# A scaled addition on one core: the first load is issued as two halves, on two queues

## The chip, the cores and the metric

The kernel runs on one core of a Trainium2 chip. The metric is the device time of one execution in microseconds (us); lower is better. For comparisons the median of several executions is taken. Besides, one execution was recorded by the hardware profiler; its span runs from the core's first instruction to its last.

## What is computed

```python
B, S, D = 512, 32, 640          # x, fx: bfloat16 of shape (B, S, D); alpha: bfloat16 of shape (1,)

def reference(x, fx, alpha):
    return x + alpha * fx
```

Each of x, fx and the output has 512 x 32 x 640 = 10,485,760 elements, 20.97 MB in bfloat16. So 41.94 MB are read from the device memory (HBM) and 20.97 MB are written.

## The kernel before

The three arrays are looked at as one flat row of elements. With K = 128 elements and P = 128 partitions (the rows of the on-chip memory), the data have 640 blocks of K x P elements, and they are cut into three chunks, of blocks 0 to 254, 254 to 464 and 464 to 640 (`CHUNKS`, L18). Within a chunk each partition holds one contiguous stretch; `rows` (L64) gives the piece of it that belongs to blocks a to b. A transfer of blocks a to b therefore has 128 rows, one for each partition, of (b - a) x 128 x 2 bytes: 8 KiB for blocks 0 to 32, 56,832 bytes for blocks 32 to 254, 65,024 bytes for blocks 0 to 254.

On chip there is a single buffer `buf` of 828 blocks (L77). The pieces of fx and x have fixed places in it (`F` and `X`, L20 and L21; `at`, L83), some of which are used twice, so that a later piece can be loaded only when an earlier one has been used up. One short piece of the product is kept in the accumulator memory (`held`, L78).

The order of the work is written out by hand in `PLAN` (L26 to L49), one step a line, and the loop at L145 issues the steps in that order:

- `f a b` and `x a b` load blocks a to b of fx and x into `buf` (`load_f`, `load_x`, both by `transfer`, L94). Every transfer is issued by the sync engine (SP) on its own DMA queue; L95 is therefore the line of all loads and stores in the profile.
- `a` (L126) loads alpha, spreads it to all partitions with a matmul by ones on TensorE, and copies it to `a_f` on VectorE (L134).
- `m a b` multiplies a piece of fx by alpha in place (VectorE, L111), `p` copies a piece of the product to `held` (L117), `t a b` adds the product to x in place (L124).
- `s a b` stores a finished chunk (SP, L95).

At the top of the plan stand `f 0 32`, the load with the 8 KiB rows, and `f 32 254`, the rest of the first chunk of fx; then alpha, `x 0 254`, `f 254 464` and the first multiply `m 0 254`, which needs both pieces of fx. SP takes its transfers in the order of the plan and waits, before one of them, for the semaphores of what must be over. At the end SP waits for all steps in `done` (L151 to L153).

The change touches the first line of the plan, the functions beside `load_f` and the table `does` (L136).

Of the kernel before, what the change touches and what calls it, by code (L numbers as in the profile page):

```python
# [1 line left out]

# [4 lines left out]

ACT = mybir.ActivationFunctionType
ALU = mybir.AluOpType
F32 = mybir.dt.float32  # L10
BF16 = mybir.dt.bfloat16
U32 = mybir.dt.uint32

K = 128
P = 128


CHUNKS = [(0, 254), (254, 464), (464, 640)]  # L18

F = [(0, 254, 464), (254, 464, 254), (464, 640, 442)]  # L20
X = [(0, 254, 0), (254, 464, 618), (464, 640, 266)]  # L21

HELD = (400, 464)
ALL = 828

PLAN = """  # L26
f 0 32
f 32 254
a
x 0 254  # L30
f 254 464
m 0 254
t 154 254
x 254 464
t 0 154
m 400 464
p 400 464
m 254 400
f 464 640
t 266 400  # L40
x 464 640
m 464 640
t 254 266
t 400 464
s 0 254
t 464 640
s 254 464
s 464 640
"""  # L49
LATE = {"s 0 254": "t 400 464"}  # L50


@with_exitstack
def kernel(
    ctx: ExitStack,
    tc: tile.TileContext,
    x: bass.AP,
    fx: bass.AP,
    alpha: bass.AP,
    out: bass.AP,  # L60
):
    nc = tc.nc

    def rows(t, a, b):  # L64

        flat = t.rearrange("b s d -> (b s d)")
        s, e = next(c for c in CHUNKS if c[0] <= a and b <= c[1])
        v = flat[s * K * P : e * K * P].rearrange("(p n) -> p n", p=P)
        return v[:, (a - s) * K : (b - s) * K]

    consts = ctx.enter_context(tc.tile_pool(name="consts", bufs=1))
    psum = ctx.enter_context(tc.tile_pool(name="psum", bufs=1, space=bass.MemoryType.PSUM))
    whole = ctx.enter_context(tc.tile_pool(name="whole", bufs=1))
    ctx.enter_context(tc.manual_schedule())

    sync = mybir.DependencyInfo(mybir.DependencyClass.Sync, mybir.DependencyReason.DATA)
    buf = whole.tile([P, ALL * K], x.dtype, name="buf")  # L77
    held = psum.tile([P, (HELD[1] - HELD[0]) * K // 2], U32, name="held")  # L78
    done = []
    said = {}  # L80
    lanes = {}

    def at(pieces, a, b):  # L83

        s, _, h = next(p for p in pieces if p[0] <= a < p[1])
        e, _, g = next(p for p in pieces if p[0] < b <= p[1])
        assert h - s == g - e
        return buf[:, (a + h - s) * K : (b + h - s) * K]

    def in_psum(a, b):  # L90
        assert HELD[0] <= a and b <= HELD[1]
        return held[:, (a - HELD[0]) * K // 2 : (b - HELD[0]) * K // 2]

    def transfer(name, out, in_):  # L94
        r = nc.sync.dma_start(out=out, in_=in_)  # L95
        if name in LATE:
            tc.add_manual_dep(r.ins, said[LATE[name]].ins.name, sync, reason="issue late")
        return r

    def load_f(a, b):  # L100
        return transfer(f"f {a} {b}", at(F, a, b), rows(fx, a, b))

    def load_x(a, b):
        return transfer(f"x {a} {b}", at(X, a, b), rows(x, a, b))

    def store(a, b):
        return transfer(f"s {a} {b}", rows(out, a, b), at(X, a, b))

    def multiply(a, b):
        term = at(F, a, b)  # L110
        return nc.vector.tensor_scalar(  # L111
            out=term, in0=term, scalar1=lanes["a_f"][:], scalar2=None, op0=ALU.mult
        )

    def hold(a, b):

        return nc.vector.tensor_scalar(  # L117
            out=in_psum(a, b), in0=at(F, a, b).bitcast(U32), scalar1=0, scalar2=None, op0=ALU.bitwise_or
        )

    def total(a, b):
        s = at(X, a, b)
        term = in_psum(a, b).bitcast(x.dtype) if HELD[0] <= a < HELD[1] else at(F, a, b)
        return nc.vector.tensor_tensor(out=s, in0=s, in1=term, op=ALU.add)  # L124

    def alpha_to_lanes():  # L126
        a_1 = consts.tile([1, 1], alpha.dtype, name="a_1")
        done.append(nc.sync.dma_start(out=a_1[:], in_=alpha[None, :]))  # L128
        ones = consts.tile([1, P], alpha.dtype, name="ones")
        nc.vector.memset(ones[:], 1.0)  # L130
        a_ps = held[:, 0:1].bitcast(F32)
        done.append(nc.tensor.matmul(a_ps, ones[:], a_1[:], start=True, stop=True))  # L132
        lanes["a_f"] = consts.tile([P, 1], F32, name="a_f")
        return nc.vector.tensor_copy(out=lanes["a_f"][:], in_=a_ps)  # L134

    does = {  # L136
        "f": load_f,
        "x": load_x,
        "a": alpha_to_lanes,
        "m": multiply,  # L140
        "p": hold,
        "t": total,
        "s": store,
    }
    for step in PLAN.split("\n"):  # L145
        if step:
            what, *of = step.split()
            said[step] = does[what](*map(int, of))
            done.append(said[step])

    rest = nc.sync.nop(nofuse=True)  # L151
    for i in done[:-1]:
        tc.add_manual_dep(rest.ins, i.ins.name, sync, reason="all but the last store")  # L153


# [1 line left out]
_INS = ['x', 'fx', 'alpha']  # L157
_OUTS = [((512, 32, 640), 'bfloat16')]


# [23 lines left out]
```

## Time and profile before

| | us |
|---|---|
| median of 3 executions | 150.68 (150.58 to 150.79) |
| the profiled execution, its own time | 150.84 |
| its span | 149.1 |
| VectorE (DVE) busy | 70.1 |
| share of the 16 DMA engines' span in packets | 98.0% |
| first load (8 KiB rows): issue by SP begins | 0.72 |
| the same: median from issue to landing | 4.8 |
| first multiply on VectorE begins | 22.70 |
| last store issued | 112.0 |

The page gives for each engine the time in which it executed instructions, for the DMA queues their packets and bytes, and the chain of work that ended last. Issuing a DMA does not count as busy; its queue is shown as SPq. A packet of a transfer is one row of one partition here, and the trace holds a record with start, duration and size for each. The time from issue to landing of a transfer contains its stay behind earlier transfers in the same queue.

### The profile page before, as it was taken

The page shows a single profiled execution, that of the slowest core. Times are in us where ns is not written, and L with a number is a line of the kernel's source. Part 1 is how long each engine was busy: PE and PEld are TensorE (multiplying, and loading weights), DVE is VectorE, ACT ScalarE, POOL GpSimd, SP SyncE. Part 2 cuts the span into 40 slices and gives each one's busy share as a digit, 9 for nine tenths or more (in the row PEclk, how much of TensorE's full clock was granted, in tenths as well). Part 3 has the DMA queues.
Part 4 walks back from the last instruction along what each step waited for, and adds up shares of the span by engine and source line. Part 5 has one row for each costly group of instructions (what it writes and reads, how often), then busy time and mean ns, then how long its engine had stood idle before and what let it go on. Part 6 is the DMA issues. An engine that isn't in the chain of part 4 may idle for free.

```text
span 149.1 us, 80 instructions
## 1 busy us (share of the span) xinstructions
PE 0.2 (0%) x1; PEld 0.1 (0%) x1; DVE 70.1 (47%) x13; POOL 0.2 (0%) x4
## 2 busy tenths in 40 slices
PE   0000000000000000000000000000000000000000
PEld 0000000000000000000000000000000000000000
DVE  0000009940089999999399179949990000000000
POOL 0000000000000000000000000000000000000000
DMA  5979996969969999999988899899696999879984
GB/s 158 611 320 412 488 523 279 558 279 558 452 303 447 462 462 462 462 462 418 430 387 387 387 532 435 387 473 558 279 558 279 510 462 462 390 315 556 399 387 193
DMA packets 1442, 62.92 MB, mean 422 GB/s; under 512 B 162, under 2 KB 162, under 8 KB 162
## 3 DMA queue, kind: packets, MB, share of 16 engines
q1 hardware_dynamic: 1442, 62.92, 98.0%
HBM read 41.94 MB, written 20.97 MB: 422 GB/s over the span
## 4 chain that ended last, share of the span: by engine, by line
DMA 55%; DVE 19%; SPq 1%; issue 0%; DVEq 0%
DMA buf<-in_x_dram 55%; DVE buf L124 19%; SPq L95 1%; SPq L128 0%; DVEq L124 0%
## 5 line engine op out<-in xcount | busy, mean ns | idle before, releaser
L124 DVE TENSOR_TENSOR buf<-buf 128x12800 bf16<-128x12800 bf16 (+4 forms) x5 | 39.1, 7836 | 15.2 <-DMA buf<-in_x_dram 15.2
L111 DVE TENSOR_SCALAR buf<-buf,a_f 128x32512 bf16<-128x32512 bf16 (+3 forms) x4 | 22.2, 5549 | 4.2 <-DMA buf<-in_fx_dram 4.2
L134 DVE COPY a_f<-held 128x1 f32<-128x1 f32 x1 | 0.2, 157 | 21.5 <-PE held L132 21.5
L117 DVE TENSOR_SCALAR held<-buf 128x4096 uint32<-128x4096 uint32 x1 | 4.4, 4428 | 0.0
L124 DVE TENSOR_TENSOR buf<-buf,held 128x8192 bf16<-128x8192 bf16 x1 | 4.4, 4414 | 0.0
L130 DVE MEMSET ones<- 1x128 bf16 x1 | 0.2, 165 | 0.8 <-PEq L168 0.8
L132 PE MATMUL held<-a,ones 1*128 1x1 bf16 x1 | 0.2, 158 | 22.3 <-DMA a<-in_alpha_dram 22.3
L168 POOL MEMSET const-bfloat16-1.0<- 128x1 bf16 x1 | 0.1, 101 | 0.0
L168 POOL MEMSET const-uint8-127<- 128x1 uint8 x1 | 0.1, 101 | 0.0
L132 PEld LDWEIGHTS <-ones 1*128 1x128 bf16 x1 | 0.1, 100 | 1.0 <-DVE ones L130 1.0
L168 POOL MEMSET const-float32-0.0<- 128x1 f32 x1 | 0.1, 98 | 0.2 <-issue 0.2
L168 POOL MEMSET const-float32-1.0<- 128x1 f32 x1 | 0.1, 98 | 0.0
## 6 DMA issues: line engine op xcount, KB each, us to landing
buf<-in_x_dram SPq DMA_DIRECT2D x1, 8128.0 KB, 39.5
out_dram<-buf SPq DMA_DIRECT2D x1, 8128.0 KB, 21.2
buf<-in_fx_dram SPq DMA_DIRECT2D x1, 7104.0 KB, 21.2
buf<-in_fx_dram SPq DMA_DIRECT2D x1, 6720.0 KB, 55.0
buf<-in_x_dram SPq DMA_DIRECT2D x1, 6720.0 KB, 24.8
out_dram<-buf SPq DMA_DIRECT2D x1, 6720.0 KB, 36.6
buf<-in_fx_dram SPq DMA_DIRECT2D x1, 5632.0 KB, 21.1
buf<-in_x_dram SPq DMA_DIRECT2D x1, 5632.0 KB, 17.4
```

The costliest lines, as they stand in the source:

```text
L95: r = nc.sync.dma_start(out=out, in_=in_)
L111: return nc.vector.tensor_scalar(out=term, in0=term, scalar1=lanes["a_f"][:], scalar2=None, op0=ALU.mult)
L117: return nc.vector.tensor_scalar(out=in_psum(a, b), in0=at(F, a, b).bitcast(U32), scalar1=0, scalar2=None, op0=ALU.bitwise_or)
L124: return nc.vector.tensor_tensor(out=s, in0=s, in1=term, op=ALU.add)
L130: nc.vector.memset(ones[:], 1.0)
L132: done.append(nc.tensor.matmul(a_ps, ones[:], a_1[:], start=True, stop=True))
L134: return nc.vector.tensor_copy(out=lanes["a_f"][:], in_=a_ps)
L168: nc = _bacc.Bacc("TRN2", target_bir_lowering=False, num_devices=1)
```

## The change

The first load of the plan becomes a step of its own kind, `2f 0 32`. It issues the rows of partitions 64 to 127 on ScalarE's DMA queue and those of partitions 0 to 63 on the sync engine's, as before. Both are in the list of what SP waits for at the end. The bytes, their places in `buf` and all other steps are the same. ScalarE has no other work in this kernel.

```diff
 PLAN = """
-f 0 32
+2f 0 32
 f 32 254
 a
 x 0 254
...
+    def load_f_by_two(a, b):
+
+        h = P // 2
+        done.append(nc.scalar.dma_start(out=at(F, a, b)[h:], in_=rows(fx, a, b)[h:]))
+        return nc.sync.dma_start(out=at(F, a, b)[:h], in_=rows(fx, a, b)[:h])
+
...
     does = {
         "f": load_f,
+        "2f": load_f_by_two,
         "x": load_x,
```

## The prediction

> **What bounds the kernel now.** I read four views in this order: the page's busy times and DMA parts, the chain that ended last, the waits of SP's queue with the waits of the engines, and the first five microseconds cut into half-microsecond stretches.
>
> From the page:
>
> ```profile
> PE 0.2 (0%) x1; PEld 0.1 (0%) x1; DVE 70.1 (47%) x13; POOL 0.2 (0%) x4
> ...
> q1 hardware_dynamic: 1442, 62.92, 98.0%
> HBM read 41.94 MB, written 20.97 MB: 422 GB/s over the span
> ```
>
> No engine is busy for half of the span, but the 16 DMA engines are, taken together, busy for 98.0% of 149.1 us. The chain of waits starts with SP's issues and then consists of DMA landings, with VectorE between them:
>
> ```profile
> 0.66 0.07 issue
> 0.72 0.38 SPq L95
> ...
> 1.99 39.54 DMA buf<-in_x_dram
> ```
>
> The first transfer is issued 0.72 us after the start. After that the chain is no help for this change: the VectorE steps in it run while the DMA engines work on other transfers. The packet records of the trace say it better. Sorted by their ends, they fall into 16 unbroken strings, one for each DMA engine, and in each the next packet begins within a few ns of the last one's end: 8 rows of 8 KiB, then 8 rows of every later transfer. A 56,832-byte row takes 2.09 us from start to start, a 65,024-byte row 2.40 us, an 8 KiB row 0.306 us. The strings begin between 1.73 and about 2.3 us and end between 147.45 and 147.98 us. So **the time is the start of a string, plus 80 rows at a fixed pace, plus about 2.9 us of landing, wind-up and what lies outside the span** (150.84 us was the profiled execution's own time, against a last end of 147.98). Only what makes a string start later, run slower or stand still can move the end.
>
> The rest of the page bears this out. VectorE first needs the first 8 KiB rows when alpha is there:
>
> ```profile
> PE held L132 <- DMA a<-in_alpha_dram: 22.3, 1, 22.3
> DVE a_f L134 <- PE held L132: 21.5, 1, 21.5
> ...
> SPq L95 <- DVE buf L124: 70.9, 4, 26.1
> ```
>
> Those rows land by 5.54 us (the landing records), so they have 17 us to spare. SP waits 70.9 us for VectorE before later issues, yet no string shows a gap there, so these waits are covered. All these VectorE steps hang on landings, so they move with the strings if these start earlier or later.
>
> What is left is the start. In the stretches the columns are the stretch, its length, four engines, PE's clock, DMA share and GB/s; a packet is counted whole where it begins, which is why shares over 1 occur:
>
> ```profile
> 1.50:2.00 0.50, 0.00 (x0) 0.00 (x0) 0.00 (x0) 0.00 (x0) 1.00 1.30 213
> 2.00:2.50 0.50, 0.00 (x0) 0.00 (x0) 0.00 (x0) 0.00 (x0) 1.00 0.64 115
> 2.50:3.00 0.50, 0.00 (x0) 0.00 (x0) 0.00 (x0) 0.00 (x0) 1.00 0.59 229
> 3.00:3.50 0.50, 0.00 (x0) 0.00 (x0) 0.00 (x0) 0.00 (x0) 1.00 1.00 426
> ```
>
> From 3 us on the rate is 426 GB/s; before that the engines hold packets but move few bytes. In the records the first row of an engine takes 0.37 to 1.29 us, a later one 0.309. Eight rows begun at 1.73 us and at the full pace would be done at 1.73 + 8 x 0.306 = 4.18 us; the strings reach that point between 4.77 and 5.17 us. So **the start loses 0.6 us on the quickest engine and 1.0 us on the slowest**. That is all the change can win.
>
> **The change part by part.**
>
> SP's issue. The number of SP's issues stays 11. The first took 0.378 us for 128 rows and alpha's, of one element, 0.315, so half the rows save 0 to 0.06 us of SP's time. The next issue ended at 1.58 us and its packets began at 4.81 us, behind the first rows: nothing waits for the 0.06 us. I put it at 0.
>
> ScalarE's issue. One instruction of 0.32 to 0.61 us (the range of SP's issues) on an engine that has nothing else; the trace releases ScalarE from the start barrier at 0.66 us, as it does SP. Its rows can therefore begin at about 1.73 us, as SP's. Cost 0.
>
> Completions. Every engine now signs off two transfers instead of one. Such a 4-byte packet takes 9 ns and some 6 ns around it: 0.015 us on every string, on the path.
>
> Waits. The first multiply now waits for two landings instead of one, and SP's last gathering wait for one more. Behind the multiply stands all of VectorE's work, but the cover is 17 us (above). SP's gathering steps take 0.06 us each and are over at 135 us, 13 us ahead of the end. Cost 0; without this cover, 0.06 us.
>
> The start. Two queues may hand the engines their first rows sooner. Bounds: 0 (what is slow at the start is the first read, which stays) and -1.0 us (the slowest engine loses nothing). The spread of the first starts, some 0.5 us, is the only part that shows engines waiting for a row to be handed out; halving it gives about -0.25 us. I take -0.2, the nearest to that row.
>
> Which engine moves which row. This is the part that the diff does not show. Now 128 rows lie on 16 engines, 8 each, and the even pace of all 16 says that none of them stands in another's way. After the change each half has 64 rows; if it is still spread over all 16 engines, each has 4 rows of the lower half and 4 of the upper, so that the 8 partitions which one engine fills now are filled by two. If the place where the rows land takes one row at a time at the present pace, two engines share it while they work on the same half. No row of the trace shows two engines at one place, so I bound it: at best the two alternate (one in the lower half while the other is in the upper) and it costs 0; at worst they stay in step, and each row lasts twice as long: 8 x 0.306 = 2.45 us. The first row is slow anyhow, which leaves 7 x 0.306 = 2.14 us as the usual worst. An engine that starts late by a part of a row stays late by that part, since both lose the same; starts differ by 0 to 0.5 us, thus by anything between no row and a whole one, and the middle is 7 x 0.153 = 1.07 us. The slowest of the 16 sets the end and would lie above the middle; engines that fall out of step on the way would lie below it. I take +1.1.
>
> [...]
>
> Sum: 0 + 0 + 0.015 + 0 - 0.2 + 1.1 = +0.9 us. Against the profiled execution that is 150.84 + 0.9 = 151.74; that execution lies 0.16 us above the median of the runs (150.68), so the forecast for the median is **151.6 us**, +0.6%. With the bounds of the sharing (0.3 to 2.3 us net) the slower case runs from 151.0 to 152.9.
>
> **The rivals.**
>
> A, faster: the start is bound by the handing out of rows, and two queues do it at once. For it: the strings begin up to 0.5 us apart, and one engine or another stands still after its first row (a gap of 0.04 to 0.24 us in the records). Against it: most of the loss sits in the first row's own 0.37 to 1.29 us, and later issues show no such loss. It decides if no two engines get in each other's way. Price: half of the slowest engine's 0.98 us, -0.49: 150.84 - 0.49 = 150.35, or 150.2 beside the median; at most 149.7.
>
> B, no change: the same 16 engines move the same 1 MB at the same pace, and the first read is as slow as now; the second queue only saves issue time that nobody waits for. For it: the string's pace of 0.306 us a row, and 0.98 us at the start of which little is shown to be handing out. Price: +0.015, so 150.7. [...]
>
> C, the second queue comes late: ScalarE's rows appear only after SP's four, and take turns with rows of 56,832 bytes. Nothing stands still, since SP's next issue is queued by 1.58 us; the sharing then touches four rows of an engine: 0 to 4 x 0.306 = 1.22 us, taken in the middle +0.6: 151.3.
>
> **How the numbers follow.** A measurement of this kernel can tell about 0.2% (0.3 us) from no change, so same is 150.38 to 150.98. Forecast (sharing outweighs the start) 0.55, all of it slower; A 0.22, faster; B 0.18, same; C 0.05, 0.03 of it slower and 0.02 same. That makes faster 0.22, same 0.20, slower 0.58. The range: of the forecast's case about a tenth may lie over 152.8, of A about half under 150.2; leaving out 0.06 and 0.11, the range 150.2 to 152.8 holds about 0.83. As both signs have weight, the slower case's own range is 151.0 to 152.9.
>
> **What would show it.** Right: 8 KiB packets that take well over 0.309 us after 3 us, and strings that reach the 56,832-byte rows later than 5.17 us; the stretch 3.0 to 3.5 us under 426 GB/s; two queues in the table of queues, at the same 62.92 MB. Wrong on the sharing: 0.309 us packets from both queues. A: strings that begin within 0.25 us and reach 56,832-byte rows before 4.9 us. B: the same 4.8 to 5.2 us. C: ScalarE's packets that begin long after 1.8 us. What would upset all of them is a change at the end of the program (a second queue that lengthens the 1.8 us outside the span), which no row here shows.

## The result and the profile after

The changed kernel takes 153.07 us (median of 4 executions, 153.02 to 153.15) against 150.69 us for the one before: a ratio of 1.0159, 95% interval 1.0146 to 1.0171, thus 2.38 us slower; the two profiled executions, at 153.07 and 150.84 us, are 2.23 us apart. The forecast was 151.6 us, the range 150.2 to 152.8. The sign was right; the time lies just above the range.

The page of the changed kernel has the same work on every engine, two queues, and the same bytes:

```profile
PE 0.2 (0%) x1; PEld 0.1 (0%) x1; DVE 70.1 (46%) x13; POOL 0.2 (0%) x4
...
q1 hardware_dynamic: 1378, 62.39, 96.3%
q10 hardware_dynamic: 80, 0.52, 1.6%
HBM read 41.94 MB, written 20.97 MB: 416 GB/s over the span
```

Queue q10 is ScalarE's: 64 rows of 8 KiB and 16 completions, as many as each load of all 128 partitions left in the kernel before; so a half is still spread over all 16 engines. The engines are as busy as before (96.3 + 1.6 = 97.9%), and yet the mean rate fell from 422 to 416 GB/s. So they hold packets for as large a share of the time, but the packets take longer. Where that is shows in the first six microseconds (the stretch, its length, four engines, PE's clock, DMA share, GB/s; a packet counts whole where it begins):

```profile
1.50:2.00 0.50, 0.00 (x0) 0.00 (x0) 0.00 (x0) 0.00 (x0) 1.00 0.00 0
2.00:2.50 0.50, 0.00 (x0) 0.00 (x0) 0.00 (x0) 0.00 (x0) 1.00 1.28 246
2.50:3.00 0.50, 0.00 (x0) 0.00 (x0) 0.00 (x0) 0.00 (x0) 1.00 0.66 246
3.00:3.50 0.50, 0.00 (x0) 0.00 (x0) 0.00 (x0) 0.00 (x0) 1.00 1.26 328
3.50:4.00 0.50, 0.00 (x0) 0.00 (x0) 0.00 (x0) 0.00 (x0) 1.00 0.99 213
4.00:4.50 0.50, 0.00 (x0) 0.00 (x0) 0.00 (x0) 0.00 (x0) 1.00 1.10 229
4.50:5.00 0.50, 0.00 (x0) 0.00 (x0) 0.00 (x0) 0.00 (x0) 1.00 1.09 262
5.00:5.50 0.50, 0.00 (x0) 0.00 (x0) 0.00 (x0) 0.00 (x0) 1.00 1.07 229
5.50:6.00 0.50, 0.00 (x0) 0.00 (x0) 0.00 (x0) 0.00 (x0) 1.00 0.97 197
```

The kernel before, in the half microseconds that follow those shown with the prediction:

```profile
3.50:4.00 0.50, 0.00 (x0) 0.00 (x0) 0.00 (x0) 0.00 (x0) 1.00 1.01 426
4.00:4.50 0.50, 0.00 (x0) 0.00 (x0) 0.00 (x0) 0.00 (x0) 1.00 0.89 377
```

Two things differ from before. No packet begins before 2.0 us (the first one at 2.05 instead of 1.73), and from 3.5 us on the rate is 197 to 262 GB/s at full engines, where it was 377 to 426 until the long rows began. In the packet records 88 of the 98 rows that begin after 3 us take over 0.5 us, with a median of 0.61; before, 93 of 94 took at most 0.33 and none over 0.5. The engines come to their first 56,832-byte rows at 6.34 to 7.21 us instead of 4.81 to 5.17, and these first long rows still take 2.23 to 2.67 us. The second long rows begin at 9.01 to 9.44 instead of 6.91 to 7.26 us. From there on both kernels run alike, on the mean of the 16 engines 2.1 us apart here and 2.3 at the end; the last row ends at 150.19 instead of 147.98 us.

The means over the 16 engines say where the 2.1 us come from: the strings start 0.29 us later, the eight 8 KiB rows of an engine take 4.56 us together instead of 3.08, and its first long row takes 2.49 us instead of 2.10. So the rows of the first load lost 1.47 us, and the long rows that began while other engines were still at that load another 0.39.

Nothing else moved. The wait for alpha and SP's waits for VectorE, which answer to the lines shown of before:

```profile
PE held L138 <- DMA a<-in_alpha_dram: 24.4, 1, 24.4
DVE a_f L140 <- PE held L138: 23.6, 1, 23.6
...
SPq L95 <- DVE buf L130: 70.9, 4, 26.1
```

Alpha comes 2.1 us later, with everything behind it; VectorE is as busy, and SP waits for VectorE as long as before. The start of the chain and the two issues show one more thing that the forecast had not seen:

```profile
0.72 0.54 SPq L107
1.26 0.06 issue
1.32 0.56 SPq L95
...
2.29 41.55 DMA buf<-in_x_dram
```

```profile
0.72 0.54 SPq L107 DMA_DIRECT2D buf<-in_fx_dram  x1
0.73 0.55 ACTq L106 DMA_DIRECT2D buf<-in_fx_dram  x1
```

Each issue of 64 rows takes 0.54 to 0.55 us, where the issue of 128 rows took 0.38.

### The profile page after: what moved, and what is told of

It reads as the page before. It is cut to its first block, busy times and chain, and to the rows that moved or that the text cites. A ratio compares the mean times of both kernels' runs of the same rounds, so it can differ in the third digit from the quotient of the medians.

```text
span 151.3 us, 83 instructions
## 1 busy us (share of the span) xinstructions
PE 0.2 (0%) x1; PEld 0.1 (0%) x1; DVE 70.1 (46%) x13; POOL 0.2 (0%) x4
## 3 DMA queue, kind: packets, MB, share of 16 engines
q1 hardware_dynamic: 1378, 62.39, 96.3%
## 4 chain that ended last, share of the span: by engine, by line
DMA 55%; DVE 18%; SPq 1%; issue 0%; DVEq 0%
DMA buf<-in_x_dram 55%; DVE buf L130 18%; SPq L95 0%; SPq L107 0%; SPq L134 0%; DVEq L130 0%
## 5 line engine op out<-in xcount | busy, mean ns | idle before, releaser
L117 DVE TENSOR_SCALAR buf<-buf,a_f 128x32512 bf16<-128x32512 bf16 (+3 forms) x4 | 22.2, 5550 | 4.2 <-DMA buf<-in_fx_dram 4.2
```

What stands on the lines that cost most here:

```text
L117: return nc.vector.tensor_scalar(out=term, in0=term, scalar1=lanes["a_f"][:], scalar2=None, op0=ALU.mult)
```

## The experiments

The theory to be tested, S, is the author's supposition from the rows of the changed kernel (0.61 us instead of 0.309): a row takes about twice its time (the doubling) when all 16 engines fill one half of the partitions, 0 to 63 or 64 to 127, whatever the queue; rows taken from both halves at once keep their pace. Why a half should be slower is no part of S: no record names the engine or the partition of a row, so only the pace of rows on chosen partitions can be tested. The main rivals: the second queue costs by itself (Q), any transfer under 128 rows is slow (N), a fixed cost (F). The kernels of one group ran on the same chip, with the kernel before beside them, whose median was 150.84 us (e1 to e4), 150.95 (e5 to e8), 150.88 (e9 to e11) and 150.74 (e12). Each edit is to `load_f_by_two` or to the first lines of the plan; ratios are to the kernel before, with 95% intervals. `f` and `src` stand for `at(F, a, b)` and `rows(fx, a, b)` in the diffs, `h` for 64, `q` for 32.

**e1, both halves on SP's queue.**

```diff
-done.append(nc.scalar.dma_start(out=f[h:], in_=src[h:]))
-return nc.sync.dma_start(out=f[:h], in_=src[:h])
+done.append(nc.sync.dma_start(out=f[:h], in_=src[:h]))
+return nc.sync.dma_start(out=f[h:], in_=src[h:])
```

> Both halves of the partitions are issued by SP, one behind the other; ScalarE issues nothing. [...] Rival Q (the second queue is what costs: the engines lose time between two queues): 150.7 to 151.0 us, rows of 0.309 us.

153.37 us, ratio 1.0164 (1.0149 to 1.0179): the whole loss, without a second queue. The stretches of e1:

```profile
1.50:2.00 0.50, 0.00 (x0) 0.00 (x0) 0.00 (x0) 0.00 (x0) 1.00 0.00 0
...
4.50:5.00 0.50, 0.00 (x0) 0.00 (x0) 0.00 (x0) 0.00 (x0) 1.00 1.05 246
5.00:5.50 0.50, 0.00 (x0) 0.00 (x0) 0.00 (x0) 0.00 (x0) 1.00 1.15 262
5.50:6.00 0.50, 0.00 (x0) 0.00 (x0) 0.00 (x0) 0.00 (x0) 1.00 1.02 213
```

The rate is about half here too (213 to 262 GB/s in the stretches shown, where the kernel before had 377 to 426 until its long rows began; 87 of the 106 rows that begin after 3 us take over 0.5 us), and Q falls. By S seven rows of an engine, each 0.306 us longer, add 2.14 us to the 150.84 us of the kernel before (an estimate from its rows), 152.98 us; the time is 0.4 us above that. One point was not foreseen: the first packet comes at 2.05 us here too, with one queue. Two issues at the same time are not what makes it late; the issue itself took 0.55 us.

**e2 and e3, cut along the rows.** Each piece has all 128 partitions and 4 KiB rows; e2 uses two queues, e3 SP alone (`c` is block 16).

```diff
+# e2
+done.append(nc.scalar.dma_start(out=at(F, c, b), in_=rows(fx, c, b)))
+return nc.sync.dma_start(out=at(F, a, c), in_=rows(fx, a, c))
+# e3
+done.append(nc.sync.dma_start(out=at(F, a, c), in_=rows(fx, a, c)))
+return nc.sync.dma_start(out=at(F, c, b), in_=rows(fx, c, b))
```

> Two queues as in the change, but cut along the rows: SP issues blocks 0 to 16 and ScalarE blocks 16 to 32, each on all 128 partitions with rows of 4 KiB. Theory S: no doubling; 4 KiB rows at about half of 0.309 us, 150.7 us plus 0.3 for the later first start that the changed kernel shows (2.05 instead of 1.73 us) = 150.7 to 151.2 us. Rival Q: the loss stays, 152.5 to 153.1 us.

> The control for the cut along the rows: SP issues blocks 0 to 16 and then 16 to 32, both on 128 partitions with 4 KiB rows, no second queue. All theories: 150.6 to 151.0 us; what it differs from the two-queue form by is the price or gain of the second queue alone. If two issues at the same time are what makes the first start late, the first packet begins at about 1.73 us here and at about 2.05 us there.

e2: 150.94 us, ratio 1.0006 (0.9997 to 1.0016). e3: 151.11 us, 1.0016 (1.0006 to 1.0026), 0.1 us above its expectation. The stretches of e2:

```profile
1.50:2.00 0.50, 0.00 (x0) 0.00 (x0) 0.00 (x0) 0.00 (x0) 1.00 0.92 115
...
3.50:4.00 0.50, 0.00 (x0) 0.00 (x0) 0.00 (x0) 0.00 (x0) 1.00 1.01 418
4.00:4.50 0.50, 0.00 (x0) 0.00 (x0) 0.00 (x0) 0.00 (x0) 1.00 1.09 434
```

Two queues at the full rate (418 and 434 GB/s), first packet at 1.76 us, 4 KiB rows of 0.159 us. Nothing is lost, and nothing is won: the first long rows begin at 4.82 to 5.43 us, no sooner than before. So for this cut the second queue brings no gain of the kind that the prediction's rival A had in mind.

**e4 and e5, the same 64 rows on other partitions.** In both, one transfer has partitions 32 to 95; in e4 SP has it and ScalarE the two outer quarters, in e5 SP has all three, the middle first.

```diff
+# e4
+done.append(nc.scalar.dma_start(out=f[:q], in_=src[:q]))
+done.append(nc.scalar.dma_start(out=f[3*q:], in_=src[3*q:]))
+return nc.sync.dma_start(out=f[q:3*q], in_=src[q:3*q])
+# e5
+for lo, hi in ((q, 3*q), (0, q)):
+    done.append(nc.sync.dma_start(out=f[lo:hi], in_=src[lo:hi]))
+return nc.sync.dma_start(out=f[3*q:], in_=src[3*q:])
```

> Two queues and halves of 64 rows as in the change, but SP's half is partitions 32 to 95; ScalarE issues 0 to 31 and 96 to 127 as two transfers. [...] Rival N (a transfer of fewer than 128 rows runs slowly whatever its partitions): all rows at about 0.6 us, 152.9 to 153.4 us.

> SP alone issues partitions 32 to 95 (64 rows), then 0 to 31 and 96 to 127 (32 rows each), one behind the other; no second queue, so that the 64 middle rows run by themselves. Theory S: after the slow first ones the middle rows run at 0.309 us, the outer ones at about 0.6; half of the doubling, 150.8 + 0.3 (a 64-row issue takes 0.55 instead of 0.38 us and its first packet comes at 2.05 instead of 1.73 us) + 1.0 to 1.3 = 152.1 to 152.4 us. Rival N (short transfers are slow on any partitions): all rows about 0.6 us, 153.0 to 153.5 us.

e4: 152.23 us, ratio 1.0089 (1.0073 to 1.0104). In total that agrees with S, by which half of the doubling, 4 x 0.306 = 1.22 us, and the 0.31 us of the late start come on top of the kernel before: 152.4 us (an estimate). But the rows of both queues had means of 0.49 to 0.50 us, with the outer rows beside the middle ones, so that e4 alone doesn't tell S from N. e5 does: 152.57 us, 1.0106 (1.0091 to 1.0121), a little over what S expected. Its stretches:

```profile
3.00:3.50 0.50, 0.00 (x0) 0.00 (x0) 0.00 (x0) 0.00 (x0) 1.00 1.01 377
3.50:4.00 0.50, 0.00 (x0) 0.00 (x0) 0.00 (x0) 0.00 (x0) 1.00 0.90 377
4.00:4.50 0.50, 0.00 (x0) 0.00 (x0) 0.00 (x0) 0.00 (x0) 1.00 1.48 442
4.50:5.00 0.50, 0.00 (x0) 0.00 (x0) 0.00 (x0) 0.00 (x0) 1.00 0.78 180
5.00:5.50 0.50, 0.00 (x0) 0.00 (x0) 0.00 (x0) 0.00 (x0) 1.00 1.00 262
```

While the middle 64 rows run, until a little after 4 us, the rate is near the full one (377 GB/s in both half microseconds from 3 us on), and in the records they take 0.309 us once the first reads are over. Then the outer quarters run, at about half the rate (180 and 262 GB/s), with rows of mostly 0.48 to 0.64 us. So for a transfer of 64 rows it is not their number but which partitions they fill: N falls, S stands. The partition also fixes which stretch of fx a row is read from, and no run separates the two; but the rows lie equally far apart in fx in both halves (65,024 bytes from one partition's row to the next), so the side where they land is the likelier one. That is argued and not shown.

**e6, four quarters on SP's queue.**

```diff
+for i in range(3):
+    done.append(nc.sync.dma_start(out=f[i*q:(i+1)*q], in_=src[i*q:(i+1)*q]))
+return nc.sync.dma_start(out=f[3*q:], in_=src[3*q:])
```

> SP alone issues the first load as four transfers of 32 partitions each. [...] The late start does not stay if it belongs to transfers of 64 rows (a 32-row issue took 0.38 us and its first packet came at 1.75 us): 153.4 - 0.3 = 152.8 to 153.2 us. If the late start belongs to any transfer under 128 rows: 153.3 to 153.6 us. If only transfers of 64 rows are slow: 150.9 to 151.5 us.

152.74 us, 1.0118 (1.0103 to 1.0133), just under the 152.8 to 153.2 us of a doubling without the late start. Rows of 0.61 us (median after 3 us) and a first packet at 1.75 us; the issues take 0.39 to 0.42 us each:

```profile
0.72 1.32 SPq L107 DMA_DIRECT2D buf<-in_fx_dram  x3
2.08 0.42 SPq L108 DMA_DIRECT2D buf<-in_fx_dram  x1
```

The doubling is there, the late start is not: with 64 rows in the first transfer the first packet came at 2.05 us (the change, e1), with 32 it comes at 1.75. e6 is 1.79 us over its kernel before, e1 was 2.53; less the 0.31 of the start, e1 has 2.2, so by the medians the quarters also escape some 0.4 us of the doubling. The profiled executions show less: their last rows end at 149.83 and 150.25 us, 0.43 us apart, of which 0.30 is the start. About 0.1 us is left, and the rest may lie between the two groups of runs.

**e7 and e8, rows of 16 KiB.** The change with blocks 0 to 64 as its first load, and its control with that load whole.

```diff
-2f 0 32
-f 32 254
+2f 0 64     # e8: f 0 64
+f 64 254
```

> The change with twice the rows: blocks 0 to 64 (16 KiB a row) as two halves on two queues, the rest of the chunk after it. Theory S: the doubling grows with the bytes, 8 x 0.612 = 4.9 us less the cover of the first row, plus 0.3 for the start: 4.5 to 5.0 us over its control with the load whole. Rival F (a fixed cost of the second queue or of the half transfers): still about 2.4 us over its control.

> The control of the kernel with 16 KiB rows: blocks 0 to 64 as one transfer by SP. All theories: close to the kernel before, 150.6 to 151.3 us, as the strings have the same bytes at the same pace.

e7: 156.31 us, 1.0359 (1.0342 to 1.0377). e8: 151.17 us, 1.0013 (1.0002 to 1.0024). The difference is 5.14 us, slightly over the 4.5 to 5.0 of S; F, with 2.4, falls. Doubling the bytes adds 5.14 - 2.38 = 2.8 us to the loss, where 8 rows of 0.306 us more give 2.45. The records of e7 show a part that S did not count: each engine works off SP's four rows and two of ScalarE's, and its other two come in turn with the long rows, down to 16 us. Three long rows of each engine then take 1.97 to 2.43 us, where e8's take 1.80, together 1.2 us an engine.

**e9 and e10, rows of 2 KiB.**

```diff
-2f 0 32
-f 32 254
+2f 0 8      # e10: f 0 8
+f 8 254
```

> The change with a quarter of the rows' length: blocks 0 to 8 (2 KiB a row) as two halves on two queues. Theory S with a start of its own: the doubling is 8 x 0.077 = 0.6 us at most and lies for the most part under the slow first reads (some 1.3 us from the first packet on), which leaves the late start of 64-row transfers, 0.3 us: 0.2 to 0.8 us over its control. If the late start costs nothing by itself: 0 to 0.4 us. Rival F (a fixed cost): 2.4 us over its control.

> The control of the kernel with 2 KiB rows: blocks 0 to 8 as one transfer of 128 rows by SP. All theories: 150.6 to 151.4 us, a first packet at about 1.75 us.

e9: 151.77 us, 1.0055 (1.0040 to 1.0071). e10: 151.18 us, 1.0021 (1.0005 to 1.0037). The difference, 0.6 us, lies in the expected 0.2 to 0.8, but both scattered by 0.5 to 1.0 us and the two intervals almost touch, so this is a bound and not a size: no fixed cost near 2 us shows here. In the profiled executions (151.50 and 151.53 us) e9's first packet is 0.32 us late too (2.06 instead of 1.74), yet the last rows end at 148.56 and 148.64 us: here the late start does not show at the end.

**e11, the first load whole on ScalarE's queue.**

```diff
+return nc.scalar.dma_start(out=at(F, a, b), in_=rows(fx, a, b))
```

> The first load (8 KiB rows, all 128 partitions) is issued by ScalarE as one transfer; SP begins with blocks 32 to 254, so the two queues start at the same moment. Theory S: nothing is shared, and nothing starts late: 150.7 to 151.2 us. Rival Q (a second queue costs by itself): 152.5 us or more. If ScalarE's queue starts later than SP's: its first packet after 1.8 us, the time as before, since SP's rows fill the gap. If two queues shorten the start: under 150.5 us.

151.66 us, 1.0048 (1.0034 to 1.0061): above what was expected, below Q. Both queues issue at 0.73 us, and every 8 KiB row takes 0.309 us. SP now begins with 56,832-byte rows, and an engine's first one takes up to 3.28 us instead of 2.10, on the mean 2.57. The 8 KiB rows of the second queue come from 4.33 us on, mostly one after each long row. But this is not where the time was lost: an 8 KiB row that is an engine's first loses about as much in the kernel before (its 16 earliest rows take 0.80 us on the mean instead of 0.309), and when each engine has ended its ninth long row, at about 24 us, after the last rows of the second queue (22.2 us), the strings are on the mean 0.03 us behind the kernel before. The profiled execution (151.37 us, against 150.84) lost its time later: between 85.7 and 90 us, 21 rows of `x 464 640`, of 45,056 bytes, took 1.75 to 2.53 us instead of 1.67, on the mean 0.43 us an engine. e8 and e10, where SP alone loads 128 partitions, show some such rows too (12 and 4 of 1.70 us or more). So e11 shows no cost of a second queue at the start; why those later rows were slow is open.

**e12, four quarters on two queues.** SP has the two lower quarters, ScalarE the two upper ones.

```diff
+for eng, i in ((nc.scalar, 2), (nc.scalar, 3), (nc.sync, 0)):
+    done.append(eng.dma_start(out=f[i*q:(i+1)*q], in_=src[i*q:(i+1)*q]))
+return nc.sync.dma_start(out=f[q:2*q], in_=src[q:2*q])
```

> The change with 32-row pieces: SP issues partitions 0 to 31 and 32 to 63, ScalarE 64 to 95 and 96 to 127. The issues are quick (0.38 us), so nothing starts late, and both queues have rows from about 1.75 us on, so that an engine can alternate between a lower and an upper place. If the alternating engines fall out of step, as the prediction's middle case had it: half of the doubling, 150.9 + 1.0 = 151.6 to 152.1 us, with many rows near 0.309 us. If they stay in step: as the quarters on one queue, 152.6 to 152.9 us, rows of 0.6 us. If two queues cure the sharing altogether: 150.8 to 151.2 us.

152.17 us, 1.0099 (1.0082 to 1.0116), just over the out-of-step case. Its stretches:

```profile
2.50:3.00 0.50, 0.00 (x0) 0.00 (x0) 0.00 (x0) 0.00 (x0) 1.00 1.00 344
3.00:3.50 0.50, 0.00 (x0) 0.00 (x0) 0.00 (x0) 0.00 (x0) 1.00 0.99 377
3.50:4.00 0.50, 0.00 (x0) 0.00 (x0) 0.00 (x0) 0.00 (x0) 1.00 1.15 328
4.00:4.50 0.50, 0.00 (x0) 0.00 (x0) 0.00 (x0) 0.00 (x0) 1.00 1.06 262
```

Here the engines take rows from the two queues in turn, and between 2.5 and 4 us the rate is 328 to 377 GB/s instead of 213 to 328 in the changed kernel; most rows of the second round then take 0.45 to 0.53 us. What the prediction held for the middle case does occur, with this cut. In the changed kernel it doesn't: there each engine works off SP's four rows (from 2.05 us) before it turns to ScalarE's (the first at 3.96 us, the last of SP's ending at 4.82), so but for this change-over all 16 are in the lower half together and then in the upper half together.

## Why the prediction was right in kind and wrong in size

What bounds the kernel: right. The time is the start of the strings plus a fixed pace; the 2.1 us that the strings had lost by their second long rows came back at the end, as 2.2 us on the last one.

SP's issue (0 to -0.06 us): wrong in sign; it took 0.54 us, 0.16 longer, and whether that is part of the late start below is not shown. ScalarE's issue: in the range given for it (0.55 us), at 0.73 us as said. Completions (0.015 us): a little low; the 32 four-byte packets of the two halves took 0.013 to 0.040 us each, the 16 of the kernel before 0.009. Waits: nothing in the profile speaks against 0; the first load was still in long before its multiply, at 7.93 us at the latest against 24.78 us.

The start (-0.2 us): **wrong**. It came out at +0.31 us, from 1.73 to 2.05 us. The bounds were 0 and -1.0, so a loss was left out without a row that excludes it. e1 and e5, each with 64 rows first on a single queue, start at 2.05 and 2.08 us; e6 and e2, with 32 and 128 rows, at 1.75 and 1.76. The first issue of a queue took 0.54 to 0.55 us with 64 rows (the change, e1), 0.38 to 0.40 with 128 (the kernel before, e2, e11) and 0.39 with 32 (e12); why, the runs do not tell.

Which engine moves which row (+1.1 us): that rows go slower when the engines are in the same half was right, why they do is not shown (two engines at one place was a supposition), and **this is the step that failed most, by its size**. By the records it cost 1.9 us, 1.47 in the first load's rows and 0.39 in the first long rows; by the medians, less the start, 2.38 - 0.31 = 2.07. That this is near the 2.14 us named as the usual worst (seven rows, each doubled) is in part luck: the second rows mostly ran at the old pace, about 0.31 us, and long rows, which the prediction left out, paid for some of the rest. (That only the first row is slow was not quite right of the kernel before either: five second rows took 0.59 to 0.99 us.)

The middle was argued from engines that are out of step by a part of a row, which helps only if each engine takes rows of the two halves in turn. They did not: each worked off its four rows of the lower half before it turned to the upper one, and a lag of less than a row leaves nearly all of them in the same half. What taking turns is worth shows best between e6 and e12, the same quarters on one queue and on two: 1.79 us lost against 1.43.

Of the 1.5 us between the +0.9 of the sum and the 2.38 measured, the start makes 0.5 and the slower rows the rest. The records give a sum without a remainder term: 0.29 (start) + 1.47 (first load) + 0.39 (first long rows) = 2.15 us, and the strings are 2.13 us apart at the second long rows. A check on another kernel is e5, in total only: half of the doubling, 4 x 0.306 = 1.22, and the start, 0.33, make 1.55; measured were 152.57 - 150.95 = 1.62 us.

Rival A (faster): the changed kernel's rows went slower (0.61 us instead of 0.309), and e2, where two queues kept the full pace (4 KiB rows of 0.159 us), gained nothing: 150.94 us against 150.84. Rival B: that the same engines move the same bytes at the same pace holds for e2, not for halves by partition. Rival C: ScalarE's rows do come late, but behind SP's four rows and not behind the long ones; its price of 0.6 us was not what was paid. In e7, with longer rows, turns with the long rows do occur (down to 16 us). The range ended at 152.8 because the slower case's own upper end (152.9) was cut, and because that end had no room for a later start.

Open: why the engines drain SP's four rows first in the changed kernel and in e7, though they take rows from the two queues in turn in e11 and e12; why the first packet comes late (2.05 to 2.08 us instead of 1.73 to 1.76) behind a first issue of 64 rows; and the slow later rows of e11.

## What to carry to other kernels

In this kernel, whose DMA engines hold packets for 97.9% of the span (98.0% before), the stretch at about half the rate (197 to 262 GB/s instead of 377 to 426) was paid in full, though it lay in the first 7 us: 2.13 us were lost by the second long rows, 2.3 at the end. Its first load was better cut along the rows than across the partitions: halves 0 to 63 and 64 to 127 cost 1.59% on two queues and 1.64% on one, while the cuts along the rows cost 0.06% on two queues, not clear of noise, and 0.16% on one, no more than e8 and e10 cost with the load whole (0.13% and 0.21%). When a cost is bounded from two ends and the middle rests on an assumption about order (here, that the queues alternate), price the case without it too, and let a bound include a loss unless a row excludes one.

## What the runs showed of the hardware

- The first issue of a queue took 0.54 to 0.55 us with 64 rows (the change, e1) and 0.38 to 0.40 us with 32 or 128 (the kernel before, e2, e11, e12). An issue behind one of 64 rows could be long too: 0.56 us for 128 rows (the change), 1.20 us for 64 rows and 32 together (e5).
- Behind a first issue of 64 rows the first packet began at 2.05 to 2.08 us (the change, e1, e5, e9), behind one of 32 or 128 rows at 1.73 to 1.76 us (the kernel before, e2, e6, e10).
- 64 rows on partitions 32 to 95, by themselves (e5), ran at 0.309 us a row of 8 KiB once the first reads were over; on partitions 0 to 63 and 64 to 127 (the change) the median after 3 us was 0.61 us.
- Two queues were served in turn (e11: the second queue's 8 KiB rows, from 4.33 to 22.2 us, mostly one after each long row) or four rows of one queue first (the change: SP's four from 2.05 to 4.82 us, ScalarE's from 3.96 us on; e7, where the last two of the other queue's four came in turn with long rows, down to 16 us).
- The 16 earliest rows took about 0.5 us more than later ones on the mean, at 8 KiB (0.80 instead of 0.309 us, the kernel before) as at 56,832 bytes (2.57 instead of 2.10, e11, up to 3.28).
